# The result of a soft mixture of experts built in token order, and stored from 128 partitions at once

## The chip, the cores and the metric

The kernel runs on one core of one Trainium2 chip. The metric is the device time of one execution in microseconds. Times are medians of several runs; a profile is one more execution, recorded by the hardware profiler.

## The reference

Block attention (8 batches, 8 heads, 576 tokens, head width 64, chunks of 64 tokens) is followed by a soft mixture of 8 experts with 4 slots each. All is float32.

```python
def _moe_ref(x, phi, w1, w2):            # x: 4608 x 512, the attention's output
    logits = x @ phi                     # 4608 x 32 slots
    d = softmax of logits over tokens
    slot_input = (d.T @ x).reshape(E, S_per_e, D)
    for e in range(E):
        slot_out[e] = np.maximum(slot_input[e] @ w1[e], 0.0) @ w2[e]
    c = softmax of logits over the 32 slots
    return (c @ slot_out).astype(np.float32)      # 4608 x 512
```

The change concerns the last line: each of 4608 tokens takes a weighted sum of 32 slot rows of 512 numbers. The result has 9.44 MB.

## The kernel before, in words

The kernel works in two stages. The first walks through nine "batches" of 512 tokens. Eight of them are the first 512 tokens of a sequence; the ninth, called REST, collects the last 64 tokens of all eight sequences, and stands fifth in the order `vs`. This stage computes the attention, the logits and a running softmax over tokens, and leaves the softmax over slots, `c`, in `c_all`. Meanwhile weights are loaded into 14 buffers `wa`, and later into 7 buffers `wb`.

The second stage is the expert layer: `up` (line 527), `turn`, `down` (line 562, which accumulates all experts in the bank `po`), and `spread`, which copies `po` to SBUF and multiplies by a matrix of repeated identities, so that the 32 slot rows stand four times over the 128 partitions in `ss`. `place` has turned `c_all` before, so that for each batch `cT` holds 128 partitions (four groups of 32 slots) by 128 columns.

Then `combine` runs for each batch (lines 588 to 607). Group `j` of 32 partitions (`SL` is 32) belongs to the chunks 4i+kh and 4i+2+kh, with j = 2i+kh; column halves (`HALF`) tell the two chunks apart. Four products of a 32-row strip (line 594), each with 128 x 512 results in one PSUM bank, are copied alternately by ACT (line 596) and DVE (line 598) into a staging buffer `ob`, one of the weight buffers that are no longer needed. Seven banks rotate. A product starts when its bank has been copied out.

The rows of a batch thus stand in SBUF so that a partition half holds 64 tokens of one chunk, and two neighbouring quarters of the staging buffer hold chunks that follow one another. Four transfers per batch (line 607) write them, each from 64 partitions with two runs of 2 KB per partition, 256 KB. All transfers of the kernel are issued in order by one queue, SP's; those of a batch wait for the copies of their two tiles.

Of the kernel before, what the change touches and what calls it, by code (L numbers as in the profile page):

```python
# [15 lines left out]
def kernel(  # L16
# [10 lines left out]
    nc = tc.nc  # L27
# [3 lines left out]
    B, H, S, D = q.shape  # L31
    P = 128
    CH = 64
    H2 = P // 2
    NC = S // CH
    UC = 8
# [6 lines left out]
    REST = B  # L43
    vs = list(range(B // 2)) + [REST] + list(range(B // 2, B))
# [3 lines left out]
    SL = phi.shape[1]  # L48
# [8 lines left out]
    HALF = (slice(0, H2), slice(H2, P))  # L57
# [34 lines left out]
    with ExitStack() as actx:  # L92
# [299 lines left out]
        def lane_select(wj):  # L392
            pw = pair("pw")[:, 0]
            nc.tensor.matmul(pw[:, 0:SL], lhsT=wj.rearrange("p j s -> p (j s)"), rhs=one, start=True, stop=True)
            wsel = a2.tile([P, SL], F32, tag="wsel", name="wsel", bufs=1)
            nc.vector.tensor_tensor(wsel, sel, pw[:, 0:SL], ALU.mult)
            ws = a2.tile([P, 1], F32, tag="ws", name="ws", bufs=1)
            nc.vector.tensor_tensor(ws, s_run, pw[:, 0:1], ALU.mult)
            return wsel, ws
# [75 lines left out]
        b = NL - 1  # L475
# [16 lines left out]
        ss = lane_select(wj)  # L492
# [13 lines left out]
    def bank(name):  # L506
        return ps2.tile([P, 512], F32, tag="ps", name=name)
# [70 lines left out]
    def spread():  # L578

        sp = f2.tile([P, 512], F32, tag="hr", name="sp")  # L580
        nc.vector.tensor_copy(sp, po)
        prs = bank("prs")
        nc.tensor.matmul(prs, lhsT=rep.rearrange("p g s -> p (g s)"), rhs=sp, start=True, stop=True)
        ss = f2.tile([P, 512], F32, tag="hr", name="ss")
        nc.scalar.copy(ss, prs)  # L585
        return ss

    def combine(b, ss, ob):
        ov = ob.rearrange("p (j f) -> p j f", j=4)
        cT = c_all[:, 4 * b:4 * b + 4, :].rearrange("p j s -> p (j s)")  # L590
        for j in range(4):
            rs = slice(SL * j, SL * (j + 1))
            pf = bank(f"pf_{b}_{j}")
            nc.tensor.matmul(pf, lhsT=cT[rs, :], rhs=ss[rs, :], start=True, stop=True)  # L594
            if j % 2 == 0:
                nc.scalar.copy(ov[:, j], pf)
            else:
                nc.vector.tensor_copy(ov[:, j], pf)

        if vs[b] == REST:  # L600
            rows = out.rearrange("(s x) f -> s x f", x=S)[:, UC * CH:S]
        else:
            rows = out[S * vs[b]:S * vs[b] + UC * CH].rearrange("(s x) f -> s x f", x=CH)
        for i in range(2):
            for sq in range(2):
                c = 4 * i + 2 * sq
                nc.sync.dma_start(rows[c:c + 2].rearrange("k x f -> x k f"), ov[HALF[sq], 2 * i:2 * i + 2])

    hrs = {}
    for e in range(0, E, 2):  # L610
# [10 lines left out]
    ss = spread()  # L621
    obs = free + [wt[2, e, h].rearrange("p g f -> p (g f)") for e in range(E) for h in range(2)]
    for b in range(NL):
        combine(b, ss, obs[b])
# [30 lines left out]
```

## Time and profile before

| what | value |
|---|---|
| time, three runs | 269.00, 269.04, 268.48 us (median 269.0) |
| profiled execution | 268.14 us, span of its instructions 266.4 us |
| PE, DVE, ACT, POOL busy | 77%, 51%, 48%, 2% of the span |
| DMA | 71.94 MB, mean 270 GB/s |
| HBM read, written | 61.93 MB, 9.44 MB |
| products of line 594 | 72 PE records, 12.1 us |
| copies into the staging buffers | 18 on ACT, 18 on DVE |
| stores | 36 transfers of 256 KB |

In the profile, PE is the matrix engine, PEld its weight loads, DVE, ACT and POOL the other engines, SPq the queue of SyncE that issues transfers. A row of the timeline or of the chain of waits has a start and a duration in microseconds; a row of a group of instructions has busy microseconds and mean nanoseconds behind the first bar, and idle time with what ended it behind the second. A row by stage has the stretch, its length, busy time and count for PE, PEld, DVE, ACT and POOL, and at the end the granted clock of the matrix engine, the mean busy share of the 16 DMA engines and GB/s.

### The profile page before, as it was taken

What the parts mean: (1) busy time and instruction counts of PE and PEld (TensorE: products, weight loads), DVE (VectorE), ACT (ScalarE), POOL (GpSimd) and SP (SyncE); (2) the same over time, 40 slices, a digit from 0 to 9 for tenths busy, and PEclk for the clock granted to TensorE, in tenths of its full rate; (3) what the DMA queues carried; (4) which work ended last, traced back from release to release, by engine and by line L of the source; (5) the groups of instructions that cost most, each with busy time, mean ns of one, the idle gap of its engine ahead of it and who ended that gap; (6) DMA issues with size and microseconds to landing.
All of it is one profiled execution on the core that took longest, in us unless ns stands there. A gap on an engine that the chain in (4) does not pass through costs nothing.

```text
span 266.4 us, 8773 instructions
## 1 busy us (share of the span) xinstructions
PE 204.7 (77%) x3820; PEld 146.7 (55%) x3820; DVE 136.5 (51%) x281; ACT 128.0 (48%) x210; POOL 6.5 (2%) x26
## 2 busy tenths in 40 slices
PE   7687969986898596998788998888999996960000
PEld 7576868765776575777567786655334311620000
DVE  7035756767676765578575789852300001870000
ACT  1579947755666654677565684432123000860000
POOL 1000000000000000000000000000400000000000
PEclk9799989999999999799999999999999999895555
DMA  6899999977699699999999999994599990588887
GB/s 209 237 245 370 255 283 349 283 208 178 192 271 322 186 230 242 342 282 270 308 338 261 256 274 328 393 352 180 164 359 415 407 383 12 157 271 251 264 261 216
DMA packets 72214, 71.94 MB, mean 270 GB/s; under 512 B 40944, under 2 KB 59376, under 8 KB 72176
## 3 DMA queue, kind: packets, MB, share of 16 engines
q1 hardware_dynamic: 72176, 71.38, 88.0%
q8 instruction: 30, 0.49, 0.8%
q14 instruction: 8, 0.07, 0.1%
HBM read 61.93 MB, written 9.44 MB: 268 GB/s over the span
## 4 chain that ended last, share of the span: by engine, by line
PE 46%; DMA 19%; DVE 10%; issue 6%; ACT 6%; SPq 2%; DVEq 0%; POOL 0%; ACTq 0%; POOLq 0%
DMA wa<-in_moe_w_dram 14%; PE psc L206 11%; PE px L267 6%; PE pq L189 6%; DVE xT L275 6%; DMA qn<-in_q_dram 4%; PE pd L119 4%; PE pp L361 3%; PE pt L233 3%; PE pk L166 3%; PE pf L594 3%; ACT kb L175 3%; PE pav L243 2%; PE pl L283 2%; DMA out_dram<-wa 1%
## 5 line engine op out<-in xcount | busy, mean ns | idle before, releaser
L175 ACT COPY kb<-pk 64x512 f32<-64x512 f32 x72 | 44.9, 623 | 10.2 <-PE pk L166 9.6
L206 PE MATMUL psc<-kb,qT 128*64 128x128 f32 x576 | 37.7, 282 | 9.2 <-issue 3.6
L206 PEld LDWEIGHTS psc<-kb,qT 128*64 128x64 f32 x576 | 32.7, 141 | 12.1 <-issue 4.2
L216 DVE TENSOR_REDUCE mx<-psc 128x16 f32<-128x1024 f32 x18 | 22.0, 1222 | 16.5 <-PE psc L206 16.5
L193 ACT COPY qT<-pq 128x1024 f32<-128x1024 f32 x18 | 18.2, 1012 | 25.1 <-PE pq L189 25.0
L275 DVE COPY xT<-px 128x1024 f32<-128x1024 f32 x16 | 19.6, 1223 | 17.6 <-PE px L267 17.6
L189 PE MATMUL pq<-ident,qn 64*64 64x64 f32 (+1 forms) x576 | 22.5, 229 | 7.9 <-DMA qn<-in_q_dram 3.9
L243 PE MATMUL pav<-vb,at 64*64 64x65 f32 x1152 | 23.3, 222 | 5.5 <-issue 4.0
L189 PEld LDWEIGHTS pq<-ident,qn 64*64 64x64 f32 (+1 forms) x576 | 19.5, 128 | 13.9 <-issue 7.3
L255 DVE TENSOR_TENSOR xs<-pav,rc 128x512 f32<-128x512 f32 x36 | 24.9, 691 | 1.2
L236 ACT COPY at<-pt 128x1024 f32<-128x1024 f32 x18 | 18.2, 1012 | 14.2 <-PE pt L233 14.1
L243 PEld LDWEIGHTS pav<-vb,at 64*64 64x64 f32 x1152 | 19.6, 134 | 9.1 <-issue 5.7
L219 DVE TENSOR_TENSOR sc<-psc,mx 128x1024 f32<-128x1024 f32 x18 | 21.9, 1218 | 0.4
L267 PE MATMUL px<-ident,xs 128*128 128x128 f32 x144 | 21.5, 295 | 0.6 <-DVE xs L255 0.5
L225 ACT ACTIVATE sc<-sc 128x1024 f32<-128x1024 f32 x18 | 19.0, 1056 | 2.1 <-DVE sc L219 2.1
L267 PEld LDWEIGHTS px<-ident,xs 128*128 128x128 f32 x144 | 16.9, 150 | 4.0 <-issue 2.2
L166 PE MATMUL pk<-ident,kn 64*128 64x64 f32 x288 | 12.7, 228 | 2.7 <-DMA kn<-in_k_dram 1.8
L527 PE MATMUL ph<-wa,siT 128*32 128x512 f32 x112 | 14.3, 594 | 0.0
L562 PE MATMUL po<-wa,hz 128*32 128x512 f32 x88 | 12.9, 595 | 0.9 <-DMA wa<-in_moe_w_dram 0.7
L166 PEld LDWEIGHTS pk<-ident,kn 64*128 64x128 f32 x288 | 10.5, 140 | 4.5 <-ACT at L236 1.9
L233 PE MATMUL pt<-ident,sc 64*128 64x64 f32 x288 | 12.8, 229 | 0.2 <-ACT sc L225 0.2
L594 PE MATMUL pf<-ss,c_all 32*128 32x512 f32 x72 | 12.1, 727 | 0.7 <-ACT ss L585 0.7
(87 smaller groups left out, 196.9 us busy)
## 6 DMA issues: line engine op xcount, KB each, us to landing
wa<-in_moe_w_dram SPq DMA_DIRECT2D x50, 512.0 KB
vb<-in_v_dram SPq DMA_DIRECT2D x64, 128.0 KB
kn<-in_k_dram SPq DMA_DIRECT2D x15, 512.0 KB
qn<-in_q_dram SPq DMA_DIRECT2D x15, 512.0 KB
wb<-in_moe_w_dram SPq DMA_DIRECT2D x14, 512.0 KB
out_dram<-wb SPq DMA_DIRECT2D x24, 256.0 KB
out_dram<-wa SPq DMA_DIRECT2D x12, 256.0 KB
kn<-in_k_dram SPq DMA_DIRECT2D x8, 128.0 KB
```

What stands on the lines that cost most here:

```text
L166: nc.tensor.transpose(out=pt[:, i, o:o + H2], in_=src[rs, h, 2 * j:2 * j + 2, :].rearrange("p j d -> p (j d)"), identity=ident[rs, rs])
L175: nc.scalar.copy(kbs[n % 2][HALF[a]].rearrange("x i hp c a (p j u) -> x a u (i hp) c p j", j=2, u=2)[:, a, u], pv[HALF[u], a].rearrange("x ...
L189: nc.tensor.transpose(out=pt[0:D * (1 + a), i, o:o + H2], in_=src[rs, f - D * a:f + D], identity=ident[rs, rs])
L206: nc.tensor.matmul(pp[HALF[sq], i, 256 * hp:256 * (hp + 1)].rearrange("p (a k x) -> p a k x", a=2, k=2)[:, :, kh], lhsT=qT[:, i, hp, CH * ...
L216: nc.vector.reduce_max(mx, psum["s"].rearrange("p i (r x) -> p (i r) x", x=CH), axis=AX.X)
L219: nc.vector.tensor_tensor(sc.rearrange("p i h (kh x) -> p (i h kh) x", x=CH), psum["s"].rearrange("p i (r x) -> p (i r) x", x=CH), psum["m ...
L233: nc.tensor.transpose(out=pt[:, sq, o:o + CH], in_=sc[rs, i, h, :], identity=ident[rs, rs])
L243: nc.tensor.matmul(pp[HALF[sq], kh, (D + 1) * h:(D + 1) * (h + 1)], lhsT=at[rs, sq, i, h, :], rhs=vb[n % NV][rs, h, i, sq, :], start=True, ...
L255: nc.vector.tensor_tensor(xs[b % 2][:, 2 * i:2 * i + 2, HG * D * g:HG * D * (g + 1)].rearrange("p k (h d) -> p k h d", d=D), av[..., 0:D], ...
L267: nc.tensor.transpose(out=psum["x"][:, hp, P * j:P * (j + 1)], in_=xs[b % 2][:, j, f:f + P], identity=ident)
L275: nc.vector.tensor_copy(d, r)
L594: nc.tensor.matmul(pf, lhsT=cT[rs, :], rhs=ss[rs, :], start=True, stop=True)
```

## The change

A PSUM tile `j` now holds 128 tokens that follow one another: chunk 4i+2sq in its lower 64 partitions and chunk 4i+2sq+1 in its upper 64, with i, sq = j // 2, j % 2. It takes two products with 64 columns of weights each, of the strips 2i and 2i+1, into the two partition halves of one bank. The copies stay. The staging buffer then holds token 128 j + p in quarter j of partition p. The first batch is stored by four transfers of 128 partitions (256 KB, each after its copy), the seven other whole batches by one transfer of 1 MB with four runs of 2 KB per partition, and REST by two transfers of 64 partitions with four runs each (512 KB).

```diff
         for j in range(4):
-            rs = slice(SL * j, SL * (j + 1))
+            i, sq = j // 2, j % 2
             pf = bank(f"pf_{b}_{j}")
-            nc.tensor.matmul(pf, lhsT=cT[rs, :], rhs=ss[rs, :], start=True, stop=True)
+            for kh, hs in enumerate(HALF):
+                rs = slice(SL * (2 * i + kh), SL * (2 * i + kh + 1))
+                nc.tensor.matmul(pf[hs, :], lhsT=cT[rs, HALF[sq]], rhs=ss[rs, :], start=True, stop=True)
...
-        if vs[b] == REST:
-            rows = out.rearrange("(s x) f -> s x f", x=S)[:, UC * CH:S]
+        seq = vs[b]
+        if seq == REST:
+            rows = out.rearrange("(c k x) f -> k x c f", k=2, x=S)
+            for kh, hs in enumerate(HALF):
+                nc.sync.dma_start(rows[kh, UC * CH:S], ov[hs])
         else:
-            rows = out[S * vs[b]:S * vs[b] + UC * CH].rearrange("(s x) f -> s x f", x=CH)
-        for i in range(2):
-            for sq in range(2):
-                c = 4 * i + 2 * sq
-                nc.sync.dma_start(rows[c:c + 2].rearrange("k x f -> x k f"), ov[HALF[sq], 2 * i:2 * i + 2])
+            js = [slice(0, 4)] if b else [slice(j, j + 1) for j in range(4)]
+            for s in js:
+                nc.sync.dma_start(
+                    out[S * seq + P * s.start:S * seq + P * s.stop].rearrange("(j p) f -> p j f", p=P), ov[:, s])
```

## The prediction

> **What bounds the kernel now.** I read the page's slices first, to see which part of the span belongs to the change.
>
> ```profile
> span 266.4 us, 8773 instructions
> PE   7687969986898596998788998888999996960000
> DMA  6899999977699699999999999994599990588887
> GB/s 209 237 245 370 255 283 349 283 208 178 192 271 322 186 230 242 342 282 270 308 338 261 256 274 328 393 352 180 164 359 415 407 383 12 157 271 251 264 261 216
> ```
>
> A slice is 6.66 us. The last five (from 233 us) hold almost no matrix work and the DMA engines at eight or nine tenths: the kernel ends in a pure store. The chain of waits, asked for 222 us to the end, and the DMA queue's timeline give the borders:
>
> ```profile
> 225.08 7.36 PE pf L594 x35
> ...
> 232.77 3.73 DMA out_dram<-wa
> ```
> ```profile
> 227.63 11.07 SPq L607 DMA_DIRECT2D out_dram<-wa  x12
> 238.81 23.60 SPq L607 DMA_DIRECT2D out_dram<-wb  x24
> ```
>
> The first product of the result starts at 225.08, the first store is issued at 227.63, the last of 36 issues ends at 262.4. Is the store held back by issuing, by producing or by moving? The table by stage answers:
>
> ```profile
> 200.00:206.00 6.00, 6.00 (x57) 2.93 (x49) 0.57 (x4) 2.03 (x4) 0.00 (x0) 1.00 1.03 416
> 206.00:212.00 6.00, 6.00 (x60) 1.82 (x56) 0.00 (x0) 0.00 (x0) 0.00 (x0) 1.00 1.02 406
> 225.10:228.80 3.70, 3.70 (x19) 2.26 (x22) 1.51 (x3) 1.33 (x3) 0.00 (x0) 0.55 0.00 0
> 229.60:230.50 0.90, 0.90 (x11) 0.78 (x7) 0.90 (x2) 0.86 (x3) 0.00 (x0) 1.00 1.00 200
> 232.00:236.00 4.00, 4.00 (x30) 1.95 (x28) 4.00 (x8) 3.92 (x7) 0.00 (x0) 1.00 0.85 267
> 244.00:248.00 4.00, 0.00 (x0) 0.00 (x0) 0.00 (x0) 0.00 (x0) 0.00 (x0) 0.50 0.85 261
> 260.00:264.00 4.00, 0.00 (x0) 0.00 (x0) 0.00 (x0) 0.00 (x0) 0.00 (x0) 0.50 0.90 266
> 264.00:266.40 2.40, 0.00 (x0) 0.00 (x0) 0.00 (x0) 0.00 (x0) 0.00 (x0) 0.50 0.34 119
> ```
>
> The last three columns are granted clock, DMA share and GB/s. While weights are loaded (128 partitions, 4 KB runs) the 16 engines are full at 406 to 416 GB/s: 4096 x 16 / 416 x 1.03 = 162 ns for a run of 4 KB. Stores move runs of 2 KB. In the stretch 229.6 to 230.5, when only the first transfers, one 64-partition half at a time, are on their way, the engines are just as full and move 200 GB/s: 2048 x 16 / 200 = 164 ns for half as many bytes. Later, with transfers of both halves in flight, a run costs 2048 x 16 / 267 x 0.85 = 104 ns. So a transfer out of 64 partitions runs at half speed (I read it as pairs of engines sharing one way into the 64 partitions), and alternating halves hides part of that. The engines are also idle 10 to 15% of the time.
>
> **The change part by part.**
>
> *Products and copies.* A copy takes 587 ns on ACT and 682 on DVE, and the two alternate:
>
> ```profile
> L598 DVE COPY wb<-pf 128x512 f32<-128x512 f32 x12 | 7.3, 682 | 0.0
> L596 ACT COPY wb<-pf 128x512 f32<-128x512 f32 x12 | 7.0, 587 | 0.1
> L594 PE MATMUL pf<-ss,c_all 32*128 32x512 f32 x72 | 12.1, 727 | 0.7 <-ACT ss L585 0.7
> ```
>
> Now a tile comes every 0.30 us, paced by the copies, which stay as they are. There are 72 PE records for 36 products, so a product is two passes; its 512 columns take the same time whether 128 or 64 result rows come out. The change makes 72 products, 144 passes, each on its own 32 rows. A pass lasts 0.43 us at full clock, since the group of four passes of the expert layer restarts at that step:
>
> ```profile
> 210.31 0.13 PEld L562 LDWEIGHTS po<-wa,hz 128*32 128x32 f32 x4 [0.30 <-issue]
> 210.74 0.13 PEld L562 LDWEIGHTS po<-wa,hz 128*32 128x32 f32 x4 [0.30 <-issue]
> ...
> 225.08 0.31 PEld L594 LDWEIGHTS pf<-ss,c_all 32*128 32x128 f32 x8 [1.56 <-ACT ss L585]
> 225.08 2.59 PE L594 MATMUL pf<-ss,c_all 32*128 32x512 f32 x11 [0.73 <-ACT ss L585]
> ...
> 226.83 0.59 ACT L596 COPY wa<-pf 128x512 f32<-128x512 f32 x1 [1.80 <-PE pf L594]
> ```
>
> The row at 225.08 shows eight weight loads, two passes of four products, within 0.31 us: products on different 32-row strips do not wait for one another. In a batch each strip now has four passes instead of two, so four tiles take 4 x 0.43 = 1.7 us, a megabyte per 1.7 us. The store needs 2.6 to 2.8 us per megabyte, which hides this from the second batch on. If the strips did not overlap beyond a pair, a tile would take 0.86 us; that is a rival below.
>
> At the start the cover is missing. The clock is at half until about 228.9 (0.55 in the row of 225.1 to 228.8). The first tile comes as today: 225.08 to 226.83, two slow passes. The second shares its strips and comes 1.7 us later, at 228.5; the third and fourth between 226.8 (full overlap) and about 229.5 (they start when the second's passes do and the queue moves on). With a copy of 0.68 the first batch is done at 229.2 to 230.3. It goes out in four pieces, so it keeps the DMA engines partly busy meanwhile and is off the sum. Batch two adds 1.7 us: 230.9 to 232.0.
>
> The two products of a tile come from different row strips and write different halves of one PSUM bank; no run shows that. The trace's nearest row is the one at 225.08, four strips into four banks at once. The Trainium skill (TensorEngine Tiling (Array Packing), Gotcha 1: PSUM Pressure) says that different row tiles cannot use the same bank at the same time; by that rule the halves of a tile take turns, which gives the first rival's pace if the other two strips still overlap, and the fourth's if they don't.
>
> *Stores.* Removed are 36 transfers of 64 partitions x 2 runs, added 4 of 128 x 1, 7 of 128 x 4 and 2 of 64 x 4. SP's order before and after, result rows in batch order (wa and wb are freed weight buffers used as staging):
>
> ```order
> L607 DMA out_dram<-wa_90 64x2x512 x4
> L607 DMA out_dram<-wa_91 64x2x512 x4
> L607 DMA out_dram<-wa_92 64x2x512 x4
> L607 DMA out_dram<-wb_3426 64x2x512 x4
> L607 DMA out_dram<-wb_3427 64x2x512 x4
> ```
> ```order
> L610 DMA out_dram<-wa_90 128x512 x4
> L610 DMA out_dram<-wa_91 128x4x512
> L610 DMA out_dram<-wa_92 128x4x512
> L610 DMA out_dram<-wb_3426 128x4x512
> L606 DMA out_dram<-wb_3427 64x4x512 x2
> ```
>
> Only the fifth batch, wb_3427, keeps 64-partition transfers. On PE each tile's product becomes two:
>
> ```order
> L594 MATMUL pf_0_3675<-ss,c_all 128x512
> L594 MATMUL pf_1_3678<-ss,c_all 128x512
> L594 MATMUL pf_2_3681<-ss,c_all 128x512
> L594 MATMUL pf_3_3684<-ss,c_all 128x512
> L594 MATMUL pf_0_3691<-ss,c_all 128x512
> ```
> ```order
> L597 MATMUL pf_0_3675<-ss,c_all 64x512 x2
> L597 MATMUL pf_1_3679<-ss,c_all 64x512 x2
> L597 MATMUL pf_2_3683<-ss,c_all 64x512 x2
> L597 MATMUL pf_3_3687<-ss,c_all 64x512 x2
> L597 MATMUL pf_0_3695<-ss,c_all 64x512 x2
> ```
>
> The pairs alternate between strips 0 and 1 for two tiles, then 2 and 3. Issuing is no limit: a load of 128 x 4 runs takes SP 450 ns at best, as the first row shows, against 595 for each of the 36 stores; what lies above is waiting for room in the queue.
>
> ```profile
> L138 SPq DMA_DIRECT2D kn<-in_k_dram x17: 450/997/3352, 0.7 to 138.0; - x17
> L607 SPq DMA_DIRECT2D out_dram<-wb x24: 595/721/1384, 238.8 to 261.8; - x24
> ```
>
> The new wait, a megabyte for four copies instead of half a batch for two, has only later stores queued behind it on SP, and they need later copies anyway. From issue to the first bytes pass 1.3 us (227.63 to about 228.9: the row of 225.1 to 228.8 moves nothing, that of 229.6 is full). So batch two flows from 232.2 to 233.3; I take 232.8.
>
> From there eight batches of 1.049 MB follow. Seven are 128-partition transfers; no row has such a store, the nearest for speed are the loads at 406 to 416 GB/s (2.5 us each), and the other end is today's 266 (3.9 us). I take 2.75 us (381 GB/s), near the loads, because a 2 KB run at 162 / 2 = 81 ns would be the same rate and only more completions per byte lie between: 19.3 us; I use 17.6 to 21.0 for the range. The fifth batch stays on halves, now with 16 runs per engine before the half changes: 5.2 us at the 200 GB/s row, 3.9 at 266, and 2.7 if both halves overlapped fully; I take 4.5.
>
> *The end.* From 264.0 on 119 x 2.4 = 0.286 MB are left, 1.1 us at 266 GB/s; from there to the end pass 1.3 us, which stays.
>
> *The sum.* 232.8 + 19.3 + 4.5 + 1.3 = 257.9 us against the span of 266.4: 8.5 us less. The profiled execution took 268.1 with that span and the median of three is 269.0, so the forecast is 269.0 - 8.5 = 260.5 us. The ends: 232.2 + 17.6 + 2.7 + 1.3 = 253.8 (time 256.4) and 233.3 + 21.0 + 5.2 + 1.3 = 260.8 (263.4).
>
> **The rivals.**
>
> 1. *PE becomes the bound.* If a tile's two products run together but nothing overtakes the second tile on the same strips, a tile takes 0.86 us (the same if the products of a tile take turns and the two pairs of strips overlap: eight passes, 3.4 us, for four tiles): 225.1 + 36 x 0.86 + 1.7 for the slow clock = 257.8, then copy 0.7, 1.3 to flow, 2.7 for the last megabyte and 1.3: 263.8, time 266.4. Against it stands the row at 225.08, where four products' second passes do not hold back the others. Chance 8%.
>
> 2. *Nothing but small change.* If HBM takes writes no faster than 266 GB/s: 232.8 + 8.39 / 0.266 + 1.3 = 265.6, time 268.2. For it: the store's slices stay at 251 to 271. Against: 200 and 267 GB/s within a few microseconds with the engines equally loaded, a limit that moves with the halves. Chance 6%.
>
> 3. *Slower: the four runs of a partition collide in HBM.* One partition's runs lie 256 KB apart (128 rows of 2 KB), where they lay 128 KB apart. If every run costs the 164 ns of the row at 229.6, the eight batches take 8.39 / 0.200 = 42 us: 276.1, time 278.7. It decides below 8.39 / (266.4 - 1.3 - 232.8) = 260 GB/s. Today's 128 KB step shows no such loss beyond the halves. Chance 4%. The Trainium skill (DMA: Bandwidth & Descriptors, Latency and other measured facts) reports 207 GB/s for copies whose rows lie 512 KiB apart from partition to partition; here partitions lie 2 KB apart and no run shows that case.
>
> 4. *Slower: the halves of a tile take turns and nothing else overlaps.* Four passes one after another are 1.72 us per tile: 225.1 + 61.9 + 1.7 + 6.0 = 294.7, time 297.3. It decides above 0.93 us per tile ((266.4 - 6.0 - 1.7 - 225.1) / 36). Chance 2%.
>
> That the transfers are not merged is excluded by SP's order above.
>
> **How the numbers follow.** The forecast has 80%, the rivals 8, 6, 4 and 2. The range 256.4 to 266.5 holds nearly all of the forecast and the first rival. A measurement of this kernel can tell about 0.2%, 0.5 us. Rival 2's gain of 0.8 us is near that, so half of its chance counts as no change. Faster: 80 + 8 + 3 = 91%; same 3%; slower 6%.
>
> **What would show each step right or wrong.** DMA share near 1 at 370 to 410 GB/s from about 234 us on, with one dip to 200 to 270 in the fifth batch; last copy near 244 us, well before the end; a copy's idle time ended by PE, not PE's by copies. Wrong are the halves if the rate stays near 266 with full engines, and the overlap of strips if the last copy comes after 255 us.

## The result, and the profile after

The changed kernel took 260.2 us (median of four runs, 259.3 to 261.5) against 269.0 for the kernel before on the same chip: a ratio of 0.968, with an interval of 0.962 to 0.975. The forecast was 260.5. Ratios leave out executions that took over 1.5% more than the fastest of the same kernel, while medians count them all, and where too few are left a ratio and its interval are not given.

In the page after, two slices of the store stand out from those of before: they move 371 to 373 GB/s.

```profile
span 259.1 us, 8888 instructions
PE   7588969989789598799989998869899999799500
DMA  6999999996599698999899999999279999049997
GB/s 207 305 244 366 252 265 338 236 275 182 159 272 293 136 321 172 288 289 355 236 271 341 261 314 288 349 400 342 99 219 319 419 404 400 27 162 373 273 371 283
```

The table by stage, with the columns explained above, shows the rates within the store:

```profile
230.00:231.00 1.00, 1.00 (x16) 0.48 (x12) 0.61 (x2) 0.59 (x1) 0.00 (x0) 1.00 0.77 287
231.00:232.00 1.00, 1.00 (x14) 0.43 (x10) 0.97 (x2) 0.69 (x2) 0.00 (x0) 1.00 1.03 383
232.00:233.00 1.00, 1.00 (x14) 0.37 (x10) 0.57 (x2) 0.67 (x2) 0.00 (x0) 1.00 0.96 359
233.00:234.00 1.00, 1.00 (x16) 0.51 (x10) 1.00 (x2) 0.79 (x2) 0.00 (x0) 1.00 0.71 264
236.00:238.00 2.00, 2.00 (x24) 0.92 (x22) 1.39 (x3) 1.21 (x3) 0.00 (x0) 1.00 1.02 375
242.00:244.00 2.00, 1.06 (x12) 0.18 (x4) 1.57 (x4) 1.17 (x2) 0.00 (x0) 1.00 0.99 197
244.00:246.00 2.00, 0.00 (x0) 0.00 (x0) 0.34 (x1) 0.00 (x0) 0.00 (x0) 1.00 1.02 246
246.00:248.00 2.00, 0.00 (x0) 0.00 (x0) 0.00 (x0) 0.00 (x0) 0.00 (x0) 0.52 0.98 297
250.00:252.00 2.00, 0.00 (x0) 0.00 (x0) 0.00 (x0) 0.00 (x0) 0.00 (x0) 0.50 1.04 399
```

From 236 us on the engines are busy for 0.97 or more of every stretch until 257 us (a share above 1 means that an engine's records overlap), and a run of 2 KB, the piece that one partition writes to one row, takes 2048 x 16 / 399 x 1.04 = 85 ns where it took 104. The dip from 242 to 248 us is the fifth batch, REST, with its two transfers of 64 partitions. The share below 1 at 230 and at 233 us is the start: batches are not ready yet.

The products start at 227.34 here and at 225.08 before; the code ahead of them is the same. In the profiles of this study that point lies between 222.3 and 228.1 us, with no order by kernel. So what a kernel does to the store is read below from the first product to the end of the span: 41.3 us before, 31.8 after, 9.5 us less, of which the span shows 7.2.

```profile
227.34 4.14 PE L597 MATMUL pf<-ss,c_all 32*64 32x512 f32 x36 [0.73 <-ACT ss L585]
228.46 0.59 ACT L599 COPY wa<-pf 128x512 f32<-128x512 f32 x1 [1.17 <-PE pf L597]
229.07 2.27 SPq L610 DMA_DIRECT2D out_dram<-wa  x4
229.32 1.29 DVE L601 COPY wa<-pf 128x512 f32<-128x512 f32 x2 [3.89 <-PE pf L597]
229.38 0.59 ACT L599 COPY wa<-pf 128x512 f32<-128x512 f32 x1 [0.33 <-PE pf L597]
230.17 0.59 ACT L599 COPY wa<-pf 128x512 f32<-128x512 f32 x1 [0.21 <-PE pf L597]
```

The copies now wait for PE (what stands in the brackets), as expected. A batch of four tiles comes every 1.72 us: the first tiles of two batches are copied at 228.46 and 230.17.

The trace has a record of each run that an engine moved. Summed over the result's 4608 runs, divided by 16 engines, they give the time that the engines were busy; what is left of the time from the first byte to the last is idle. All in microseconds, from one profile each, as are all such figures below:

| kernel | first product to first byte | first to last byte | engines busy | idle | first product to end |
|---|---|---|---|---|---|
| before | 3.9 | 36.2 | 31.3 | 4.9 | 41.3 |
| after | 2.6 | 28.1 | 27.2 | 0.8 | 31.8 |

So the 9.5 us are 4.0 of shorter runs, 4.1 of idle time and 1.3 of an earlier first byte. As much was gained in idle time as in the speed of a run.

The 104 ns of before are a mean of two kinds of run, which the same records tell apart. Before, 69% of the runs take 100 ns or less, 85 on average, as runs do after the change; 24% take 130 ns or more, around 160. In the first microsecond, when only the first transfer flows, out of one half, 93% take 140 ns or more. After the change 89% take 100 ns or less and 8% take 130 or more, and with the fifth batch whole too (an experiment below) it is 95% and 1%. So alternating halves does not shorten each run by a part: about seven in ten take as long as any run after the change, and one in four takes about twice that.

Two explanations were to be told apart: that a transfer spans 128 partitions, or that 13 transfers stand where 36 stood.

### The profile page after: what moved, and what is told of

Read it like the earlier page. It is cut to its first block, busy times and chain, and to the rows that moved or that the text cites. A ratio compares the mean times of both kernels' runs of the same rounds, so it can differ in the third digit from the quotient of the medians.

```text
span 259.1 us, 8888 instructions
## 1 busy us (share of the span) xinstructions
PE 211.0 (81%) x3892; PEld 147.4 (57%) x3892; DVE 137.1 (53%) x281; ACT 128.4 (50%) x210; POOL 6.5 (3%) x26
## 4 chain that ended last, share of the span: by engine, by line
PE 49%; DMA 21%; ACT 7%; DVE 7%; issue 6%; SPq 3%; DVEq 0%; POOL 0%; ACTq 0%; POOLq 0%
DMA wa<-in_moe_w_dram 15%; PE psc L206 10%; PE px L267 7%; DMA qn<-in_q_dram 6%; PE pf L597 6%; PE pq L189 6%; DVE xT L275 5%; ACT kb L175 4%; PE pd L119 4%; PE pp L361 3%; PE pt L233 3%; PE pk L166 3%; PE pl L283 2%; PE ph L527 2%; PE pav L243 2%
## 5 line engine op out<-in xcount | busy, mean ns | idle before, releaser
L206 PE MATMUL psc<-kb,qT 128*64 128x128 f32 x576 | 38.8, 287 | 8.5 <-ACT qT L193 3.2
L206 PEld LDWEIGHTS psc<-kb,qT 128*64 128x64 f32 x576 | 33.6, 144 | 11.8 <-ACT qT L193 3.5
L243 PE MATMUL pav<-vb,at 64*64 64x65 f32 x1152 | 24.2, 227 | 8.2 <-issue 6.3
L243 PEld LDWEIGHTS pav<-vb,at 64*64 64x64 f32 x1152 | 20.4, 138 | 11.9 <-issue 8.0
L267 PE MATMUL px<-ident,xs 128*128 128x128 f32 x144 | 20.5, 287 | 0.0
L267 PEld LDWEIGHTS px<-ident,xs 128*128 128x128 f32 x144 | 16.2, 146 | 3.1 <-issue 1.9
L597 PE MATMUL pf<-ss,c_all 32*64 32x512 f32 x144 | 15.7, 589 | 0.7 <-ACT ss L585 0.7
L527 PE MATMUL ph<-wa,siT 128*32 128x512 f32 x112 | 16.0, 661 | 0.0
L361 PE MATMUL pp<-xs,eN 128*32 128x512 f32 x72 | 11.3, 604 | 1.6 <-issue 1.3
```

Source lines behind the costliest of these rows:

```text
L206: nc.tensor.matmul(pp[HALF[sq], i, 256 * hp:256 * (hp + 1)].rearrange("p (a k x) -> p a k x", a=2, k=2)[:, :, kh], lhsT=qT[:, i, hp, CH * ...
L243: nc.tensor.matmul(pp[HALF[sq], kh, (D + 1) * h:(D + 1) * (h + 1)], lhsT=at[rs, sq, i, h, :], rhs=vb[n % NV][rs, h, i, sq, :], start=True, ...
L267: nc.tensor.transpose(out=psum["x"][:, hp, P * j:P * (j + 1)], in_=xs[b % 2][:, j, f:f + P], identity=ident)
L527: nc.tensor.matmul(ph[SL * i:SL * (i + 1), :], lhsT=siT[:, j, :], rhs=wt[1, e, j // 2][:, j % 2, DM * h:DM * (h + 1)], start=(j == 0), sto ...
L597: nc.tensor.matmul(pf[hs, :], lhsT=cT[rs, HALF[sq]], rhs=ss[rs, :], start=True, stop=True)
```

## The experiments

Each expectation was written before the run. Ratios are to the kernel before on the same chip, with 95% intervals. The edits are against the changed kernel, unless it is said otherwise; `...` stands for lines that are left out.

**Size alone.** All whole batches go out in pieces of 256 KB, still from 128 partitions:

```diff
-            js = [slice(0, 4)] if b else [slice(j, j + 1) for j in range(4)]
+            js = [slice(j, j + 1) for j in range(4)]
```

> The changed kernel, with each of the eight whole batches stored by four transfers of 256 KB, each from 128 partitions with one run of 2 KB, behind its own copy. Theory (what counts is that a transfer spans 128 partitions, so that a run takes about 84 ns instead of 104 to 164): the store moves 380 to 400 GB/s as in the changed kernel, and the time is 259 to 261 us. Rival (what counts is a megabyte per transfer, 13 issues and completions instead of 36): with 34 transfers of 256 KB, the size and nearly the number of before, the rate falls back towards 266 GB/s and the time to 266 to 269 us.

Measured: 260.6 us, 0.971 (0.958 to 0.983); 31.7 us from the first product to the end.

```profile
230.00:232.00 2.00, 2.00 (x24) 0.95 (x20) 1.57 (x4) 1.24 (x4) 0.00 (x0) 1.00 1.03 383
232.00:236.00 4.00, 4.00 (x41) 1.63 (x34) 3.00 (x5) 2.91 (x5) 0.00 (x0) 1.00 1.03 382
248.00:252.00 4.00, 0.00 (x0) 0.00 (x0) 0.00 (x0) 0.00 (x0) 0.00 (x0) 0.50 1.02 384
```

The rate and the busy share are those of the changed kernel. With 128 partitions the size of a transfer does not matter here.

**Partitions alone.** All whole batches go out in halves, twice the size of before:

```diff
...
+            rows = out[S * seq:S * seq + 4 * P].rearrange("(j k x) f -> k x j f", k=2, x=CH)
+            for kh, hs in enumerate(HALF):
+                nc.sync.dma_start(rows[kh], ov[hs])
```

> The changed kernel, with each whole batch stored by two transfers of 64 partitions with four runs each, 512 KB, lower half first. Theory (partitions): all batches now run as the fifth one does in the changed kernel's profile, at 200 to 300 GB/s, so from the first bytes 9.44 MB take 32 to 47 us; time 266 to 282 us, most likely 270 or more, so slower than the changed kernel by 6 us at least and near or above the kernel before. Rival (size of transfers): 18 transfers of 512 KB are twice the size of before and half as many, so the time lies near the changed kernel, 260 to 263 us.

Measured: 264.6 us, 0.984 (0.972 to 0.996); 36.4 us from the first product to the end, 4.6 of them to the first byte, as a batch waits for four copies. Neither theory said that. The stages, from the first 4 us on:

```profile
228.00:232.00 4.00, 4.00 (x44) 1.83 (x42) 2.98 (x5) 2.68 (x5) 0.00 (x0) 1.00 0.99 216
232.00:236.00 4.00, 4.00 (x42) 1.71 (x38) 3.14 (x6) 2.69 (x6) 0.00 (x0) 1.00 1.02 326
248.00:252.00 4.00, 0.00 (x0) 0.00 (x0) 0.00 (x0) 0.00 (x0) 0.00 (x0) 0.50 1.03 362
```

The store begins at 216 GB/s, at first with the lower half of the first batch alone, and climbs to 362; only 0.5 us of its 30.4 are idle. A run falls from 2048 x 16 / 216 x 0.99 = 150 ns to 93 in the best stretch; over the whole store it takes 104 ns, against 109 before. So half transfers are not slow all along, and most of what this kernel gains over the one before is idle time (0.5 us instead of 4.9), not shorter runs (29.9 us busy instead of 31.3). I read the climb so: a run is slow while both engines of a pair are in the same half; given room, the engines drift apart until one is in the lower half and its partner in the upper. The records do not name an engine, so this is not shown.

**Products alone, stores alone.** The first has the new tiles with transfers of 64 partitions and two runs, the second the old products (one per tile) with the new transfers, so that rows of a batch come out in another order.

```diff
...
+        for i in range(2):
+            for kh, hs in enumerate(HALF):
...
+                nc.sync.dma_start(rows[kh, :, 2 * i:2 * i + 2], ov[hs, 2 * i:2 * i + 2])
```
```diff
...
+            rs = slice(SL * j, SL * (j + 1))
...
+            nc.tensor.matmul(pf, lhsT=cT[rs, :], rhs=ss[rs, :], start=True, stop=True)
```

> The products of the changed kernel alone: tiles in token order by two products each, stored by four transfers per batch of 64 partitions with two runs, 256 KB, as before. Theory: the products bring nothing by themselves and cost only the later first tiles, 0 to 1.5 us, and the store runs at 255 to 270 GB/s: 268.5 to 270.5 us. Rival (the products themselves bring time, by the order in which the tiles come): well below 268 us.

> The stores of the changed kernel with the products of before, one per tile; the rows of a batch come out in another order in it. Theory: nearly the whole gain is here, and a little more than in the changed kernel, as tiles come every 0.30 us instead of 0.43: 258.5 to 260.5 us. Rival (the products share in the gain, or the slower pace of the tiles costs much): above 262, or below 257.5 us.

Measured: the products alone 269.2 us, 1.010 (1.006 to 1.014), and 41.0 us from the first product to the end where the kernel before has 41.3, so the 1% does not show in this stretch of the profile. The rates are those of before:

```profile
234.00:238.00 4.00, 4.00 (x40) 1.69 (x36) 3.14 (x6) 2.70 (x6) 0.00 (x0) 1.00 0.87 270
254.00:258.00 4.00, 0.00 (x0) 0.00 (x0) 0.00 (x0) 0.00 (x0) 0.00 (x0) 0.50 0.90 266
```

The stores alone 260.4 us, 0.969 (0.957 to 0.982); 31.1 us from the first product to the end. The products bring nothing themselves, and their slower pace costs 0.7 us (31.8 less 31.1; the engines are idle 0.03 us here and 0.8 in the changed kernel). Both measured times lie where the theories put them.

**Where the idle time was.** The sum of issues less the runs already moved, at the end of each issue, shows how much is outstanding: about 340 runs in the kernel before, 2.7 of its transfers; about 550 with halves of 512 KB, 2.1; up to 1,814 after, 3.5. So the queue holds about two to three and a half transfers, whatever their size. My theory was that, if an engine of a pair falls behind, the queue is held by it and the others run dry, the sooner the smaller the transfers. To test that on the kernel before, the second tile pair of each batch goes through ACT's queue; the edit, against the kernel before, is this alone:

```diff
...
+                queue = nc.scalar if i else nc.sync
+                queue.dma_start(rows[c:c + 2].rearrange("k x f -> x k f"), ov[HALF[sq], 2 * i:2 * i + 2])
```

> The kernel before, with the transfers of the second tile pair of each batch issued by ACT's queue instead of SP's, so that twice as many transfers can be outstanding; size, partitions and alternation stay. In the profile of before the 16 engines are busy 31.3 us of the 36.2 from the first to the last byte, and at most about 350 runs (2.7 transfers) are outstanding. Theory (the idle 4.9 us come from a queue that holds few transfers while the engines of a pair slow one another unevenly): idle falls to 1 to 2.5 us and the time from the first product to the end from 41.3 to 37.5 to 39.5 us. Rival (idle is part of a 64-partition transfer, whatever the queue): 40.8 us or more.

Measured: 265.5 us (259.9 to 267.3, with no interval); in the profile, which is of the fastest of the four executions, 35.5 us from the first product to the end, and 1.2 us idle of 30.9. How long the store took in the other three is not on record.

```profile
238.00:242.00 4.00, 4.00 (x14) 2.32 (x14) 1.81 (x4) 1.37 (x3) 0.00 (x0) 0.50 1.02 335
246.00:250.00 4.00, 0.13 (x2) 0.00 (x0) 0.69 (x1) 1.60 (x4) 0.00 (x0) 0.50 1.04 355
```

The same 36 transfers of 64 partitions, with more of them outstanding (about 420 runs instead of 340), lose most of the idle time, as the theory said. The stretch as a whole is shorter than it said (37.5 to 39.5): the runs are also 1.5 us shorter in sum (103 ns on average instead of 109, 96 at best, at 355 GB/s), and the first byte comes 0.6 us sooner; I had counted neither. The edit does more than lengthen the queue: ACT's copies now wait behind its issues, and the last copy comes 28.1 us after the first product instead of 13.3. The store ended sooner all the same.

A short queue is not enough to make engines idle: with pieces of 256 KB out of 128 partitions (the first experiment) about 290 to 370 runs are outstanding too, and 0.7 us are idle. So the idle time of before takes both, a queue of two to three transfers and transfers of 64 partitions.

**The fifth batch.** All batches are written whole, each to 512 rows of its own, so that the rows come out in another order; in the next run REST keeps its place and goes out by eight transfers of one run per partition, halves in turn.

```diff
...
+            nc.sync.dma_start(
+                out[4 * P * b + P * s.start:4 * P * b + P * s.stop].rearrange("(j p) f -> p j f", p=P), ov[:, s])
```
```diff
...
+            for j in range(4):
+                for kh, hs in enumerate(HALF):
+                    nc.sync.dma_start(rows[kh, UC * CH:S, j], ov[hs, j])
```

> The changed kernel, but every batch, the fifth too, is written to 512 rows of its own that follow one another, so that all nine go out from 128 partitions; the rows of the result come out in another order. Theory: the fifth batch costs 2.7 us instead of about 5.2, so the time from the first product to the end falls from 31.8 us (changed kernel's profile) to 29 to 29.8, and the time by 2 to 2.8 us against the changed kernel. Rival (the dip to 197 to 297 GB/s at 242 to 248 us has another reason, such as HBM or the queue): 31 to 32 us, no gain.

> The changed kernel, with the fifth batch stored by eight transfers of 64 partitions with one run each, lower and upper half in turn. Theory A (halves in flight side by side shorten a run from 164 to about 104 ns, as before): the fifth batch takes 3.4 to 4 us instead of 5.2, from the first product to the end 30.2 to 31 us. Theory B (transfers of four runs per engine are too short for the queue, which holds about three transfers, and the engines run dry): 31.5 to 33 us.

Measured: whole 257.2 us, 0.956 (0.945 to 0.967), 30.4 us from the first product to the end, so REST costs 1.4 us and not 2 to 2.8; the dip is gone (368 GB/s or more from 232 to 252 us). Alternating 260.4 us, 0.964 (0.951 to 0.978), 31.9: theory B, the engines run dry. While the eight small transfers are issued the engines are not full; at the last four of them 114 to 165 runs are outstanding, about two transfers again:

```profile
238.00:240.00 2.00, 1.28 (x12) 0.20 (x4) 1.57 (x4) 1.36 (x3) 0.00 (x0) 1.00 0.88 264
240.00:242.00 2.00, 0.00 (x0) 0.00 (x0) 0.55 (x1) 0.00 (x0) 0.00 (x0) 0.82 0.74 175
```

**The order of the tiles.** Tiles 0, 2, 1, 3 use strips 0 and 1, 2 and 3 in turn.

```diff
-        for j in range(4):
+        for j in (0, 2, 1, 3):
...
-            if j % 2 == 0:
+            if j // 2 == 0:
...
```

> The changed kernel, with the tiles of a batch made in the order 0, 2, 1, 3, so that all four strips of 32 rows start at once; ACT copies tiles 0 and 1, DVE 2 and 3. Theory (the pace of the tiles only costs at the start): the first batch is done 0.4 to 0.7 us earlier after the first product, the last copy stays at about 17 us behind it, and the time from the first product to the end is 31.2 to 31.8 us, against 31.8. Rival (the pace of 0.43 us per tile holds the store back all along): 1 us or more.

Measured: 260.8 us, 0.972 (0.961 to 0.982); 31.25 us from the first product to the end, as the theory said. The first batch is copied 0.5 us earlier, and the engines' idle time in the first 4 us of the store falls from 0.6 us to 0.1; the last copy comes 0.5 us earlier too (16.5 us), which the theory did not say. Two tiles now come at a time:

```profile
228.09 4.09 PE L597 MATMUL pf<-ss,c_all 32*64 32x512 f32 x36 [0.73 <-ACT ss L585]
229.21 0.59 ACT L599 COPY wa<-pf 128x512 f32<-128x512 f32 x1 [1.17 <-PE pf L597]
229.27 0.69 DVE L601 COPY wa<-pf 128x512 f32<-128x512 f32 x1 [3.09 <-PE pf L597]
230.07 0.59 ACT L599 COPY wa<-pf 128x512 f32<-128x512 f32 x1 [0.27 <-PE pf L597]
230.13 0.69 DVE L601 COPY wa<-pf 128x512 f32<-128x512 f32 x1 [0.17 <-PE pf L597]
```

**Put together.** With this order, the upper half of REST was issued by ACT's queue; then also the first three whole batches went out in pieces. The changed kernel ran beside them.

```diff
...
+                (nc.scalar if kh else nc.sync).dma_start(rows[kh, UC * CH:S], ov[hs])
```
```diff
...
+            js = [slice(0, 4)] if b > 2 else [slice(j, j + 1) for j in (0, 2, 1, 3)]
```

> The changed kernel with the tile order 0, 2, 1, 3 and with the upper half of the fifth batch issued by ACT's queue, so that both halves are outstanding side by side. Theory (two half transfers that are in flight together let the engines of a pair work on different halves; in series they hold each other up): the fifth batch loses less than 0.7 us against a whole one instead of 1.4, and the time from the first product to the end is 30.0 to 30.8 us (31.25 with the tile order alone). Rival (both halves at once conflict just as much, or ACT's wait for DVE's last copy delays the tiles): 31.2 us or more.

> As the run before it, and the first three whole batches go out in four pieces of 256 KB each, behind their copies, the later ones as one megabyte. Theory (once transfers span 128 partitions their size does not matter for the rate, and pieces fill the gaps of the first 3 us, where whole batches wait for four copies): 0.3 to 0.8 us less than the run before it, 29.4 to 30.3 us from the first product to the end. Rival (a megabyte per transfer matters for the rate): 0.5 us more than the run before it, or worse.

> The changed kernel once more, on the same chip as the two runs before it: 31.5 to 32.1 us from the first product to the end, and a time of 259 to 261.5 us; by the theory 0.8 to 2.2 us above the two.

Measured: 258.9 us, 0.975 (0.968 to 0.983); 257.0 us, 0.959 (0.949 to 0.969); the changed kernel 259.5 us, 0.976 (0.970 to 0.982). From the first product to the end they take 31.2, 31.25 and 31.7 us. So the first two lie 0.6 and 2.6 us below the changed kernel beside them, where 0.8 to 2.2 was expected. REST through two queues gained nothing over the order of the tiles alone (31.25 us): the rival. Its dip stays, if less deep:

```profile
240.00:242.00 2.00, 1.42 (x16) 0.26 (x8) 1.67 (x3) 1.46 (x3) 0.00 (x0) 1.00 1.03 282
242.00:244.00 2.00, 0.00 (x0) 0.00 (x0) 0.21 (x1) 0.04 (x1) 0.00 (x0) 1.00 1.01 257
```

Its runs are 0.5 us shorter in sum than with the tile order alone, and as much is lost at the end, where the engines finish one after another: in the last 2 us before the last byte 1.1 us are idle (shares of 0.76, 0.30 and 0.17 in the half microseconds from 254 us on) instead of 0.6. The pieces met neither theory. After the tile order there was no gap left at the start for them to fill (0.1 us idle in the first 4 us), and the ragged end, again 1.1 us, stays with them:

```profile
250.00:250.50 0.50, 0.00 (x0) 0.00 (x0) 0.00 (x0) 0.00 (x0) 0.00 (x0) 0.50 0.85 324
250.50:251.00 0.50, 0.00 (x0) 0.00 (x0) 0.00 (x0) 0.00 (x0) 0.00 (x0) 0.50 0.66 254
251.00:251.50 0.50, 0.00 (x0) 0.00 (x0) 0.00 (x0) 0.00 (x0) 0.00 (x0) 0.50 0.36 139
```

In the profile with the low median the first product came early (222.3 us), so the kernel ran again:

> The run with pieces first once more. Its median was 257.0 us, 2.6 below the changed kernel beside it, yet from its first product to the end it took 31.25 us against 31.7; the rest lies ahead of the first product (222.3 us into the span, where the changed kernel has 226 to 227), in code that is the same. Theory (that part varies from execution to execution and is not the change's): the profile has the first product anywhere between 222 and 228 us, again 31 to 31.6 us behind it, and the median lies at 257 to 260 us. Rival (this version starts its products earlier each time): again near 222 us, with a median at or below 257.

Measured: 260.3 us (254.6 to 262.7, with no interval), with the first product at 226.8 us and 31.3 us from it to the end. The low median did not come back; the 260.3 lies just above the 257 to 260 that were expected. No version here that writes the rows in their order beats the changed kernel by more than the 0.5 us of the tile order, which lies within the spread of its times.

## Why the prediction was right

**The sum.** Counted from the first product, the forecast's end lay at 32.8 us; measured 31.8. The span shrank by 7.2 us instead of 8.5 only because the first product came 2.3 us later, which the change does not do. That the time fell within 0.3 us of the forecast is thus partly luck: the store gained 9.5 us where 8.5 were forecast, and the stretch ahead of it differs by up to 6 us between profiles.

**The first batches** were mis-sized. I let the clock be at half as in the profile of before; in the profile after it is full there (1.00 from 227 to 229 us), so the first batch is copied 3.3 us after the first product (forecast 4.1 to 5.2) and the second flows at 6.4 us instead of 7.1 to 8.2. Part of the earlier first byte is thus the clock: the kernel before with two queues, whose clock was full there too (1.00 until 226 us), has its first byte after 3.3 us where the kernel before has it after 3.9, so about 0.6 of the 1.3 us is not the change's.

**The pace of the tiles** was right: 1.72 us per batch, last copy 17.0 us behind the first product, at 244.3. Taking turns would need 3.4 us per batch (rival 1) or more; so the halves of a tile do not take turns in their bank, and rivals 1 and 4 are out. For two row strips in different partition halves of a bank, the trace therefore differs from the Trainium skill (TensorEngine Tiling (Array Packing), Gotcha 1: PSUM Pressure), which allows different row tiles no access to one bank at a time; the same partitions were not tried.

**The eight later batches** were right in sum: 23.8 us forecast; measured about 24.3, from 233.7 (SP's issue of the second batch at 232.4 and 1.3 us) to the last byte at 258.0. REST takes 1.4 us of it more than a whole batch, so it takes about 4.3 (forecast 4.5), and a whole batch 2.9 (2.75). The rate of 399 GB/s at runs 256 KB apart rules out rivals 2 and 3.

**The reason given was only half of it.** I wrote that a transfer out of 64 partitions runs at half speed and that alternating halves hides part of that. Shown is: 93% of the runs are slow (around 160 ns) while one half alone is stored, but only 24% over the whole store of before; the best stretches come to 93 ns with halves of 512 KB and 96 with two queues, at 64 partitions still. Measured against the changed kernel, what kept the kernel before at 266 GB/s was in equal parts these slow runs (4.0 us) and engines that ran dry behind a queue of about 2.7 transfers (4.1 us). I had read off the idle 10 to 15% and given it no cause; the sum left it out without a reason of its own, because its rate came from the loads, which keep the engines full. Transfers of 128 partitions remove both at once.

The Trainium skill (SBUF — State Buffer, Door 1: The DMA port swizzle) says that 64 partitions reach only 8 of 16 ports; the trace agrees for the first stretch, 200 GB/s against 399 for 128 partitions. The same page of the Trainium skill (section "Can I just issue two DMAs to hit both halves?") says that two transfers at once, one out of each half, bring 6%; here a long queue of such transfers, lower and upper half in turn, reached 63 to 81% more (326 and 362 GB/s against 200), so for such a stream the measurement decides against it. Two transfers by themselves were not run.

That two engines of a pair share a way into 64 partitions is argued from these rates and the two lengths of a run; no record here tells one engine from another.

## What to carry to other kernels

Store from all 128 partitions, even if that costs twice the products, where the work on PE is hidden behind the store as it is here. If a long store can only go out in halves, make each transfer large (36.4 us here, against 41.3) or use a second queue (35.5 in one profile), so that the engines do not run dry. For a single batch between whole ones, as REST, neither small alternating transfers nor a second queue gained anything. Read the busy share beside the rate: time per run and idle time are two causes that one figure in GB/s mixes. And read the lengths of single runs beside their mean, which here stood for two kinds of run and was the length of neither.

## What was not expected

- The queue holds transfers, not bytes: about 340 runs outstanding with 128 per transfer, 550 with 256, up to 1,814 with 512.
- PE works on tiles of other strips out of order but reports in order. After the change the semaphore of the first tile comes at 228.44 us and those of the next three at 229.29, 229.35 and 229.41, although the third tile's passes had begun with the first's: four passes start within 0.04 us at 227.34, and the second tile has the same two strips as the first. The rows above agree: ACT's second copy and DVE's first start together, at 229.38 and 229.32.
- A run takes 89 ns in the changed kernel while PE, ACT and DVE are busy (2048 x 16 / 375 x 1.02, the row of 236 us) and 85 ns after they have stopped (399 GB/s at 1.04, the row of 250 us). It is not shown that they disturb it: with the fifth batch whole, a run takes 89 ns both while they work (377 GB/s at 1.03 from 234 to 236 us) and after they have stopped (the same from 244 to 246 us).
